# Linear attention and SwiGLU on one core: a fifth seven-product tile pair per chunk, 16-bit gating operands and a new issue order

## The chip, the cores and the metric

The kernel runs on one core of one Trainium2 chip. The metric is the device time in microseconds (us) of a whole execution. "Fast" is the state in which nearly all executions agree. Still, single executions of one kernel spread by about 1 us, and now and then one is 2 to 4 us longer at a lower granted clock. Where a median is given, the kernel before was run on the same chip. A profile shows a single execution, and not always a typical one.

## The reference

```python
# q, k, v: (8 batches, 8 heads, 576 positions, 64), fp32
q_s = softmax(q, axis=-1)                    # over the head dimension
k_s = softmax(k, axis=2)                     # over the positions
kv  = einsum('bhsd,bhse->bhde', k_s, v)
x   = einsum('bhsd,bhde->bhse', q_s, kv)     # -> 4608 tokens x 512
g   = x @ w_gate                             # 512 x 1536
u   = x @ w_val
out = (g * sigmoid(g) * u) @ w_out           # 1536 x 512, fp32
```

## The kernel before

TensorE (PE) does the matrix products. The first 576 tokens (the "head" of the program) run as plain products while batch 1's attention is made ready. "Chunk 0" has 448 tokens. Seven full chunks of 512 follow: 1 to 5 run one plan, 6 and 7 another, and a last output product ends the program.

In a chunk, gate and value tiles come in pairs of either of two forms. `Direct` does a pair of tiles with 16 matmuls of 512 columns. `Pair` does the same pair as a 2x2 block product with seven products instead of eight: 28 matmuls of 256 columns, paid for with sums of inputs (`xs`), sums of weights (`gt`), and adds and copies of its partial results on VectorE (DVE) and ScalarE (ACT). In steps `a` to `g` and `v`, `s1`, `s2` and `s5` are SBUF tiles that carry partial results:

```python
NP = 4                                  # pairs with ready weight sums
...
sn = ctx.enter_context(tc.tile_pool(name="sn", bufs=2))
...
def s_tile(self, nm):
    return sn.tile([128, 512], FP32, tag=nm, name=nm)[:, 0:2 * self.h]
...
elif step == "d":
    self.s2 = self.s_tile("s2")
    self.prod(self.x, self.sum(1), xs[1])
    copy(ceng, self.s2, self.x[:, 0:w])                        # ACT, or DVE with *
elif step == "e":
    self.prod(self.w, self.raw(wv, 1), xs[3])
    nc.vector.tensor_add(self.s2, self.w[:, 0:w], self.s2)     # in place, fp32
    meng.tensor_mul(self.out(0), self.halves(self.sa), self.halves(self.s2))  # POOL
...                                     # f and g do the same with s5
```

The gating product (`hr = silu(g) * u`) is mostly on GpSimd (POOL). The output product (`Quad`, steps A to H) uses the same seven-product form and the same tags `s1`, `s2`, `s5`, two buffers each.

The order of instructions on every engine is written by hand as a plan, a list of tokens (batch numbers start at 0, so batch 1 is the second):

```text
I, J      plain gate and value products of the head
O         half of an output product of the head, 6 matmuls of 512 columns
kk0:1     key-value product of batch 1, first half of the heads ("kv" on PE)
load:2    the last v load of the third batch, issued by SyncE (SP)
cv        cast of v on POOL      nm   norm of q on POOL, then a DMA transpose from SP
xx        the attention product "xa" of the next batch, which needs that transpose
Q, W, Y, X   sums of gate and value weights, of output weights, of this and of the next chunk's inputs
a..g,v    a Pair's steps         G, U a Direct's         a trailing * moves work to another engine
```

The head's plan and that of chunk 0 before:

```text
PLAN_B (head)
I0 I1 I2 I3 J0 J1 J2 I4 pe:1 J3 I5 I6 J4 I7 I8 J5 J6 J7 eq0:1 ns0:1 eq1:1 J8 I9 Q0
I10 I11 ek0:1 nd0:1* ns1:1 J9 J10 J11 nd1:1* O01 Q2* tr00 tr01 cv0:1 O02 tr10 Q1*
ek1:1 O11 kk0:1 O21 eq0:2 tr11 cv1:1 xz01 load:2 xz00 Q3 O12 kk1:1 ns0:2 O22 xz11*
O31 xz10 ek0:2 eq1:2 O32 nm0:2* cv0:2 cv1:2 ek1:2
PLAN_0 (chunk 0: four Pairs, two direct)
Y0 Y1 Y2 a0* G4 b0 c0 Y3* v0 G10 W0* a1 d0* U4 f0 G5 b1 ns1 c1 g0 e0 d1 v1 U10 a2
f1 nm1 e1 b2 v2 kv silu:2 g1 d2 c2 G11 f2 load e2 a3 g2 b3 c3 d3 v3 xx* W1 e3 f3
U5 U11 W3 X0 g3* X1 X2 W2 X3
```

The softmax here doesn't subtract the row's maximum and nothing guards it: scores larger than these inputs give would overflow.

Of the kernel before, what the change touches and what calls it, by code (L numbers as in the profile page):

```python
# [8 lines left out]
FP32 = mybir.dt.float32  # L9
# [7 lines left out]
def kernel(  # L17
# [19 lines left out]
    nc = tc.nc  # L37
# [10 lines left out]
    HM = MT // 2  # L48
    HN = d_model // 2
    XR = 1536  # L50
    NP = 4
    WARM = (64, 8, 8)

    const = ctx.enter_context(tc.tile_pool(name="const", bufs=1))
    ld = ctx.enter_context(tc.tile_pool(name="ld", bufs=3))
    at = ctx.enter_context(tc.tile_pool(name="at", bufs=2))
    ff = ctx.enter_context(tc.tile_pool(name="ff", bufs=4))
    ob = ctx.enter_context(tc.tile_pool(name="ob", bufs=5))
# [20 lines left out]

    def load(b, G, what, src, after=None):  # L80
        raw[what, b, G] = ld.tile(
            [128, 2, T * 64], FP32, tag=what, name=what, bufs=2 if what == "v" else 3
        )
        ap = bass.AP(
            tensor=src.tensor,
            offset=src[b, 4 * G].offset,
            ap=[[T * 64, 128], [2 * HSTR, 2], [1, T * 64]],
        )
        d = nc.sync.dma_start(out=raw[what, b, G], in_=ap)
        if after is not None:  # L90
            tc.add_manual_dep(d.ins, after.ins.name, SYNC, reason="order of loads")
        dmas[what, b, G] = d
# [207 lines left out]
    class First:  # L300
# [15 lines left out]
        def run(self, step, alt=False):  # L316
            if step == "I":
                ps = self.mm(wg, "g_ps")
                self.sg = ff.tile([128, S], FP32, tag="sg", name="sg")
                for p_, (c, n) in zip(ps, self.parts):  # L320
                    nc.scalar.activation(
                        out=self.sg[:, c:c + n], in_=p_[:, 0:n], func=AF.Silu
                    )
            else:
                for p_, (c, n) in zip(self.mm(wv, "u_ps"), self.parts):
                    nc.vector.tensor_mul(
                        hr[:, self.m, c:c + n], self.sg[:, c:c + n], p_[:, 0:n]
                    )
# [25 lines left out]
            eng.tensor_sub(s[3], a12, s[1])  # L354

    def sg_tile():
        return ff.tile([128, S], FP32, tag="sg", name="sg")

    class Pair:
        def __init__(self, c0, h, n, tsum, tc0):  # L360
# [29 lines left out]
                        start=first and j == 0 and kk == 0, stop=kk == 1, skip_group_check=True,  # L390
                    )

        def s_tile(self, nm):
            return sn.tile([128, 512], FP32, tag=nm, name=nm)[:, 0:2 * self.h]

        def run(self, step, alt=False):
            w = 2 * self.h
            ceng = nc.vector if alt else nc.scalar
            meng = nc.vector if alt else nc.gpsimd
            if step == "a":  # L400
                self.x, self.s1 = f_tile("sx"), self.s_tile("s1")
                self.prod(self.x, self.raw(wg, 0), self.xa(0, 0), True)
                copy(ceng, self.s1, self.x[:, 0:w])
            elif step == "b":
                self.y = f_tile("sy")
                self.prod(self.y, self.raw(wg, 1), self.xa(0, 1), True)
            elif step == "c":
                self.w, self.s5 = f_tile("sw"), self.s_tile("s5")
                self.prod(self.w, self.sum(0), xs[0], True)
                copy(ceng, self.s5, self.w[:, 0:w])  # L410
            elif step == "v":
                nc.vector.tensor_add(self.s1, self.y[:, 0:w], self.s1)  # L412
                self.sa = sg_tile()
                nc.scalar.activation(out=self.sa[:, 0:w], in_=self.s1, func=AF.Silu)  # L414
# [3 lines that stand above are left out]
                copy(ceng, self.s2, self.x[:, 0:w])  # L418
            elif step == "e":
                self.prod(self.w, self.raw(wv, 1), xs[3])  # L420
                nc.vector.tensor_add(self.s2, self.w[:, 0:w], self.s2)  # L421
                meng.tensor_mul(self.out(0), self.halves(self.sa), self.halves(self.s2))  # L422
            elif step == "f":
                self.prod(self.x, self.sum(2), xs[2])
                nc.vector.tensor_add(self.s5, self.x[:, 0:w], self.s5)  # L425
            elif step == "g":
                self.prod(self.x, self.sum(3), self.xa(1, 1))
                sb = sg_tile()
                nc.scalar.activation(out=sb[:, 0:w], in_=self.x[:, 0:w], func=AF.Silu)  # L429
                meng.tensor_mul(self.out(1), self.halves(sb), self.halves(self.s5))  # L430

    class Direct:
        def __init__(self, c0, n, m):
# [74 lines left out]
    class Quad:  # L508
        def __init__(self, Q, kks, own=False):
            self.Q, self.r, self.kks = Q, (512 * Q) % RING, kks  # L510
            pool = (lambda n: ld.tile([128, 512], FP32, tag=n, name="os")) if own else None
            self.s_tile = (
                (lambda n: pool("q" if n == "s1" else "k")) if own
                else lambda n: sn.tile([128, 512], FP32, tag=n, name=n)
            )
            self.o_sb = [[None, None], [None, None]]
# [83 lines left out]
    with tc.manual_schedule():  # L600
# [70 lines left out]
        def op(t, ci, c0, h, parts):  # L671
# [62 lines left out]
                g_sum(int(a), nc.vector if alt else nc.gpsimd)  # L734
            elif k == "T" and ci == B - 2:
                i = int(a)
                if i % 2 == 0:
                    parts["t"] = ld.tile(
                        [128, 2, 2, 2, 128 * (HM - NP)], FP16, tag=("q", "k")[i // 2], name="gt2"
                    )  # L740
                gt2[i] = parts["t"][:, i % 2]
                g_sum(i, nc.gpsimd if alt else nc.vector, 128 * NP, 128 * HM, gt2)

        def chunk(ci, c0, n, plan):
# [13 lines left out]
        ORDER = (0, 1, 2, 3, 4, 5)  # L758
        gt2 = [None] * 4
        PLAN_B = """  # L760
        I0 I1 I2 I3 J0 J1 J2 I4 pe:1 J3 I5 I6 J4 I7 I8 J5 J6 J7 eq0:1 ns0:1 eq1:1 J8 I9 Q0
        I10 I11 ek0:1 nd0:1* ns1:1 J9 J10 J11 nd1:1* O01 Q2* tr00 tr01 cv0:1 O02 tr10 Q1*
        ek1:1 O11 kk0:1 O21 eq0:2 tr11 cv1:1 xz01 load:2 xz00 Q3 O12 kk1:1 ns0:2 O22 xz11*
        O31 xz10 ek0:2 eq1:2 O32 nm0:2* cv0:2 cv1:2 ek1:2
"""
        PLAN_0 = """
        Y0 Y1 Y2 a0* G4 b0 c0 Y3* v0 G10 W0* a1 d0* U4 f0 G5 b1 ns1 c1 g0 e0 d1 v1 U10 a2
        f1 nm1 e1 b2 v2 kv silu:2 g1 d2 c2 G11 f2 load e2 a3 g2 b3 c3 d3 v3 xx* W1 e3 f3
        U5 U11 W3 X0 g3* X1 X2 W2 X3
"""  # L770
        PLAN = """
        S002 G4 pe a0 b0 A S222 S022 ek0 c0 S042 eq0 B S242 U4 d0 C ek1 S202 S142 eq1 v0
        S102 S122 e0 f0 a1* G10 S322 S302 D S342 b1 g0 cv0 cv1 v1 d1 ns1 E nm1 F c1 f1 a2
        U10 b2 ns0 c2 nm0 H* v2 g1 d2* e1 a3 f2 e2 b3 v3 kv c3 g2 d3 e3 G5 f3 xx X2 X0
        silu U5 G11 U11 load X1* X3 g3*
"""
        PLAN_N = """
        a0 S242 T0 b0 S022 A d0 S222 c0 v0 a1 f0 S002 S042 S102 S142 B g0 e0 d1 S122 b1 c1
        v1 a2 f1 b2 D S202 g1 T1 S302 d2 v2 e1 S322 c2 a3 f2 T2 C g2 d3 e2 b3 c3 T3* v3 f3
        a4 e3 b4 g3 d4 c4 v4 a5 S342 f4 b5 e4 g4 v5 d5* c5 E f5 e5 F g5* X0 X1 X3 X2 H*  # L780
"""
        PLAN_E = """
        S042 S002 A S102 S022 S242 S302 B C S122 S142 S322 S222 S342 D S202 E F H*
"""
        chunk(-1, 0, S, PLAN_B)
        chunk(0, S, 1024 - S, PLAN_0)
# [33 lines left out]
```

## Time and profile before

| | before |
|---|---|
| time, median of 3 runs | 298.43 us (298.03 to 298.5) |
| span of the profiled run | 296.2 us |
| head / chunk 0 / the rest / tail | 39.32 / 19.23 / 216.90 / 4.9 us |
| period of a steady chunk | 30.37 us |

The stretches are cut by PE's own instructions in the timeline. The head runs from the first plain gate product (15.89) to the first 224-column matmul of chunk 0 (55.21), chunk 0 to PE's first instruction of chunk 1 (74.44), the rest to the end of PE's last group (291.34), and the tail to the end of the span.

The page of the kernel before gives the span, then the busy time of each engine with its share and instruction count, then the shares of the chain of work that ended last:

```profile
span 296.2 us, 6921 instructions
...
PE 288.5 (97%) x2644; PEld 227.3 (77%) x2644; DVE 231.1 (78%) x496; ACT 207.2 (70%) x381; POOL 154.5 (52%) x121
...
PE 93%; DMA 3%; ACT 1%; DVE 0%; POOL 0%; issue 0%; ACTq 0%; DVEq 0%; POOLq 0%
```

PE is busy 97% of the span, and 93% of the chain is PE. The Trainium skill, "Trainium Kernel Development and Optimization", section "Performance Expectations", warns that matmul busy time is a bad metric for how close a kernel is to its bound, since matmuls are pipelined. So the bound is also checked by durations: in the steady chunk, 256-column matmuls start 0.109 us apart and 512-column ones 0.2155. "TensorE: Matmul & The Clock Gate", section "Wait — 56ns, not 53.3ns?", gives N / 2.4 GHz plus about 2.5 ns, which is 0.109 and 0.216: the trace agrees, so PE runs at its full rate there.

A steady chunk of the kernel before, by windows (start and end, length, busy us and instruction count of each engine, granted clock, DMA share, GB/s):

```profile
core 0: us, PE busy (x) PEld busy (x) DVE busy (x) ACT busy (x) POOL busy (x), PEclk, DMA share, GB/s
96.84:127.21 30.37, 30.37 (x282) 23.56 (x282) 25.45 (x56) 22.89 (x41) 16.30 (x13) 1.00 0.66 172
```

No engine but PE is full, and the clock is full. What PE waited for, over the whole of the kernel before (us in total, times, longest):

```profile
PE kv L192 <- POOL vb L118: 1.6, 1, 1.6
PE warm_ps L256 <- DVE zero L610: 1.1, 1, 1.1
```

The second is the start of the program. The first is in the head, as PE's timeline of the kernel before shows (start, us, engine, line, operation, out<-in, shapes, count, and in brackets the idle time before and what ended it):

```profile
42.91 1.46 PE L477 MATMUL o_ps<-wo,hr 128*128 128x512 f16 x6
45.95 0.70 PE L192 MATMUL kv<-vb,ek 64*128 64x129 bf16 x18 [1.59 <-POOL vb L118]
...
55.21 0.55 PE L388 MATMUL sx<-xt,wg 128*128 128x224 f16 x4
...
74.44 1.03 PE L439 MATMUL g_ps<-xt,wg 128*128 128x512 f16 x4
```

The first key-value product of batch 1 waits 1.59 us for POOL's cast of v, and the cast itself waits for a load. Chunk 0 follows at 55.21, chunk 1 at 74.44.

### The profile page before, as it was taken

Reading aid. Unit: us, or ns where it says so; the run is one execution under the profiler, and the core shown is the slowest. Engines: PE = TensorE matmul, PEld = TensorE weight load, DVE = VectorE, ACT = ScalarE, POOL = GpSimd, SP = SyncE. Lnnn points to the kernel's source line nnn. Section 1 sums busy time; section 2 is a strip of 40 time slices with the busy share of each in tenths; the row PEclk is TensorE's granted clock in tenths of the full one; section 3 lists DMA queues with packets and bytes.
Section 4 is the critical chain, followed back from the end, with each engine's and each line's share of the span. In section 5 each row is a group of like instructions: output and inputs, shape, how many; then the busy total and the mean of one; then the engine's idle time right before and its main releaser. Section 6 shows DMA issues by size and latency. Waiting matters only on the chain.

```text
span 296.2 us, 6921 instructions
## 1 busy us (share of the span) xinstructions
PE 288.5 (97%) x2644; PEld 227.3 (77%) x2644; DVE 231.1 (78%) x496; ACT 207.2 (70%) x381; POOL 154.5 (52%) x121
## 2 busy tenths in 40 slices
PE   8999997999999999999999999999999999999993
PEld 6877764587788678877887778767886888888882
DVE  2834785897997879787978798788889988787781
ACT  5667854968995589567966796679666785667441
POOL 1903737598029811991099109920893379147700
PEclk9999999999999999999999999999999999999998
DMA  7999999917705991579138913793351000600235
GB/s 261 291 190 243 244 308 362 340 25 231 289 2 109 158 395 45 90 159 393 65 73 169 388 73 74 152 342 138 73 117 36 2 0 13 133 2 0 64 80 142
DMA packets 38335, 46.43 MB, mean 157 GB/s; under 512 B 16288, under 2 KB 21408, under 8 KB 38304
## 3 DMA queue, kind: packets, MB, share of 16 engines
q1 hardware_dynamic: 32864, 41.03, 47.6%
q0 software_dynamic: 5280, 4.72, 10.1%
q8 instruction: 20, 0.33, 0.5%
q10 hardware_dynamic: 160, 0.26, 0.2%
q14 instruction: 11, 0.09, 0.1%
HBM read 37.75 MB, written 9.44 MB: 159 GB/s over the span
## 4 chain that ended last, share of the span: by engine, by line
PE 93%; DMA 3%; ACT 1%; DVE 0%; POOL 0%; issue 0%; ACTq 0%; DVEq 0%; POOLq 0%
PE sx L388 21%; PE ox L531 13%; PE sw L388 10%; PE u_ps L439 7%; PE ow L531 7%; PE g_ps L439 7%; PE sy L388 5%; PE g_ps L310 4%; PE warm_ps L256 4%; PE oy L531 4%; PE kv L192 3%; PE u_ps L310 3%; PE o_ps L477 2%; DMA v<-in_v_dram 2%; PE xa L273 1%; DMA out_dram<-o_sb 1%
## 5 line engine op out<-in xcount | busy, mean ns | idle before, releaser
L422 POOL TENSOR_TENSOR hr<-sg,s 128x512 bf16<-128x512 f32 (+1 forms) x36 | 46.0, 1284 | 63.7 <-ACT sg L414 47.0
L388 PEld LDWEIGHTS <-gt 128*128 128x128 f16 x576 | 55.7, 98 | 11.5 <-issue 1.1
L430 POOL TENSOR_TENSOR hr<-sg,s 128x512 bf16<-128x512 f32 (+1 forms) x28 | 36.2, 1292 | 21.2 <-ACT sg L429 21.0
L388 PE MATMUL sx<-xs,gt 128*128 128x256 f16 (+1 forms) x288 | 42.8, 271 | 0.1
L531 PEld LDWEIGHTS <-hs 128*128 128x128 bf16 x384 | 37.6, 98 | 5.4
L116 ACT COPY s<-sx 128x512 f32<-128x512 f32 (+1 forms) x58 | 33.7, 581 | 3.4 <-PE sx L388 2.8
L152 POOL TENSOR_TENSOR qs<-eq,rr 128x1152 bf16<-128x1152 bf16 x14 | 29.7, 2123 | 8.3 <-DVE rr L147 6.2
L388 PEld LDWEIGHTS <-wg 128*128 128x128 f16 x288 | 28.1, 98 | 6.0
L414 ACT ACTIVATE sg<-s 128x512 f32<-128x512 f32 (+1 forms) x36 | 22.6, 629 | 14.3 <-DVE s L412 12.3
L425 DVE TENSOR_TENSOR s<-sx,s 128x512 f32<-128x512 f32 (+1 forms) x36 | 24.5, 682 | 9.5 <-PE sx L388 5.5
L421 DVE TENSOR_TENSOR s<-sw,s 128x512 f32<-128x512 f32 (+1 forms) x36 | 24.4, 679 | 8.9 <-PE sw L388 4.6
L429 ACT ACTIVATE sg<-sx 128x512 f32<-128x512 f32 (+1 forms) x36 | 21.3, 592 | 13.8 <-PE sx L388 7.7
L531 PEld LDWEIGHTS <-hr 128*128 128x128 bf16 x288 | 28.2, 98 | 3.3
L116 ACT COPY s<-sw 128x512 f32<-128x512 f32 (+1 forms) x36 | 20.9, 581 | 12.5 <-PE sw L388 12.4
L412 DVE TENSOR_TENSOR s<-sy,s 128x512 f32<-128x512 f32 (+1 forms) x36 | 24.1, 669 | 1.6 <-PE sy L388 1.5
L143 DVE TENSOR_REDUCE rs<-eq 128x18 f32<-128x1152 bf16 x16 | 21.5, 1346 | 4.4 <-ACT eq L127 4.4
L439 PE MATMUL g_ps<-xt,wg 128*128 128x512 f16 (+1 forms) x96 | 24.2, 375 | 0.0
L439 PE MATMUL u_ps<-xt,wv 128*128 128x512 f16 (+1 forms) x96 | 24.1, 375 | 0.0
L531 PE MATMUL ox<-wt,hs 128*128 128x256 f16 x192 | 23.6, 273 | 0.0
L127 ACT ACTIVATE ek<-k 128x1152 bf16<-128x1152 f32 x16 | 18.8, 1172 | 6.7 <-DMA k<-in_k_dram 6.7
L127 ACT ACTIVATE eq<-q 128x1152 bf16<-128x1152 f32 x16 | 18.7, 1169 | 4.7 <-DMA q<-in_q_dram 4.7
L388 PE MATMUL sx<-xt,gt 128*128 128x256 f16 (+1 forms) x144 | 21.4, 271 | 0.1
(100 smaller groups left out, 581.7 us busy)
## 6 DMA issues: line engine op xcount, KB each, us to landing
q<-in_q_dram SPq DMA_DIRECT2D x16, 576.0 KB, 6.1
k<-in_k_dram SPq DMA_DIRECT2D x16, 576.0 KB, 6.3
v<-in_v_dram SPq DMA_DIRECT2D x16, 576.0 KB, 7.4
out_dram<-o_sb SPq DMA_DIRECT2D x70, 128.0 KB, 2.4
wv<-in_moe_w_val_dram POOLq DMA_DIRECT2D x3, 512.0 KB, 11.2
wo<-in_moe_w_out_dram POOLq DMA_DIRECT2D x3, 512.0 KB, 10.5
wg<-in_moe_w_gate_dram POOLq DMA_DIRECT2D x2, 512.0 KB, 11.2
wg<-in_moe_w_gate_dram POOLq DMA_DIRECT2D x2, 256.0 KB, 5.1
```

Of the source, the lines that this page charges most:

```text
L116: nc.scalar.copy(out=out, in_=in_)
L127: nc.scalar.activation(out=s["e" + what], in_=raw[what, b, G].rearrange("p h (t d) -> p t h d", d=64), func=AF.Exp,)
L152: eng.tensor_mul(s["qs"].rearrange("p t (h d) -> p (t h) d", d=64), s["eq"].rearrange("p t h d -> p (t h) d"), s["rr"].to_broadcast([128, ...
L388: nc.tensor.matmul(out=bank[:, h * j:h * j + h], lhsT=wgt(kk, j), rhs=rhs[:, kk, 0:h], start=first and j == 0 and kk == 0, stop=kk == 1, s ...
L412: nc.vector.tensor_add(self.s1, self.y[:, 0:w], self.s1)
L414: nc.scalar.activation(out=self.sa[:, 0:w], in_=self.s1, func=AF.Silu)
L421: nc.vector.tensor_add(self.s2, self.w[:, 0:w], self.s2)
L422: meng.tensor_mul(self.out(0), self.halves(self.sa), self.halves(self.s2))
L425: nc.vector.tensor_add(self.s5, self.x[:, 0:w], self.s5)
L430: meng.tensor_mul(self.out(1), self.halves(sb), self.halves(self.s5))
L439: nc.tensor.matmul(out=ps[:, 0:self.n], lhsT=w[:, kk, 128 * self.m:128 * self.m + 128], rhs=xt[:, kk, self.r:self.r + self.n], start=(kk = ...
L531: nc.tensor.matmul(out=dst[p][:, 0:HN], lhsT=lhs(kk, p), rhs=rhs(kk), start=start and i == 0, stop=i == HM - 1, skip_group_check=True,)
```

## The change

The intent: in chunks 0 to 5 a fifth pair takes the seven-product form, which is shorter on PE; the gating product gets two 16-bit operands, so that it is shorter on POOL and DVE; the space comes from one k buffer fewer; and all plans are written anew to fit.

```diff
-    NP = 4
+    NP = 5
@@ load
-            [128, 2, T * 64], FP32, tag=what, name=what, bufs=2 if what == "v" else 3
+            [128, 2, T * 64], FP32, tag=what, name=what, bufs=3 if what == "q" else None   # else 2
@@ sg_tile, and the same in First
-        return ff.tile([128, S], FP32, tag="sg", name="sg")
+        return ff.tile([128, S], FP16, tag="sg", name="sg")
@@ Pair
-        def s_tile(self, nm):
-            return sn.tile([128, 512], FP32, tag=nm, name=nm)[:, 0:2 * self.h]
+        def s_tile(self, nm, dt=FP32):
+            return sn.tile([128, 512], dt, tag=nm, name=nm)[:, 0:2 * self.h]
@@ step e
-                nc.vector.tensor_add(self.s2, self.w[:, 0:w], self.s2)
-                meng.tensor_mul(self.out(0), self.halves(self.sa), self.halves(self.s2))
+                u = self.s_tile("u0", FP16)
+                nc.vector.tensor_add(u, self.w[:, 0:w], self.s2)
+                meng.tensor_mul(self.out(0), self.halves(self.sa), self.halves(u))
@@ step f (step g then multiplies by self.u instead of self.s5)
-                nc.vector.tensor_add(self.s5, self.x[:, 0:w], self.s5)
+                self.u = self.s_tile("u1", FP16)
+                nc.vector.tensor_add(self.u, self.x[:, 0:w], self.s5)
@@ PLAN_B, the head
+        I0 I1 pe:1 I2 I3 J0 J1 I4 I5 J2 J3 J4 Q0 I6 J5 I7 J6 J7 eq0:1 ns0:1 eq1:1 I8
+        nd0:1* ns1:1 J8 I9 J9 I10 Q1* nd1:1* I11 cv0:1 tr00 J10 J11 tr10 ek0:1 O01 Q3*
+        cv1:1 ek1:1 O11 tr01 kk0:1 O02 tr11 eq0:2 O12 kk1:1 ns0:2 O21 xz10* ek0:2 xz00*
+        O22 Q2 xz01 eq1:2 cv0:2 xz11 O31 load:2 nm0:2 cv1:2 O32 ek1:2
@@ PLAN_0, chunk 0
+        a0 ns1 G5 b0 G11 Y0 c0 Y2 Y1 v0 Y3* d0* W2 a1 f0 b1 U5 c1 g0 d1 W0 v1 e0 a2 f1 b2
+        v2 kv silu:2 nm1 g1 d2 a3 e1 c2 f2 b3 c3 e2 g2 d3 v3 e3 a4 f3 xx* load g3 W1 d4*
+        b4 c4* X0 f4 v4 U11 e4* X2* X1 W3 X3 g4*
@@ cut: the plans of the full chunks and of the end, the tags of a wide tile and of the last Quads
```

More of the change, by code (lines that the diff above doesn't have):

```diff
@@ L50 @@
     XR = 1536
-    NP = 4
+    NP = 5
     WARM = (64, 8, 8)
     const = ctx.enter_context(tc.tile_pool(name="const", bufs=1))
-    ld = ctx.enter_context(tc.tile_pool(name="ld", bufs=3))
+    ld = ctx.enter_context(tc.tile_pool(name="ld", bufs=2))
     at = ctx.enter_context(tc.tile_pool(name="at", bufs=2))
@@ L318, in run @@
                 ps = self.mm(wg, "g_ps")
-                self.sg = ff.tile([128, S], FP32, tag="sg", name="sg")
+                self.sg = ff.tile([128, S], FP16, tag="sg", name="sg")
                 for p_, (c, n) in zip(ps, self.parts):
@@ L429, in run @@
                 nc.scalar.activation(out=sb[:, 0:w], in_=self.x[:, 0:w], func=AF.Silu)
-                meng.tensor_mul(self.out(1), self.halves(sb), self.halves(self.s5))
+                meng.tensor_mul(self.out(1), self.halves(sb), self.halves(self.u))
     class Direct:
@@ L510, in __init__ @@
             self.Q, self.r, self.kks = Q, (512 * Q) % RING, kks
-            pool = (lambda n: ld.tile([128, 512], FP32, tag=n, name="os")) if own else None
+            pool = (lambda n: ld.tile([128, 512], FP32, tag=n, name="os", bufs=3 if n == "q" else None)) if own else None
             self.s_tile = (
-                (lambda n: pool("q" if n == "s1" else "k")) if own
+                (lambda n: pool({"s1": "q", "s2": "v", "s5": "k"}[n])) if own
                 else lambda n: sn.tile([128, 512], FP32, tag=n, name=n)
@@ L736, in op @@
                 i = int(a)
-                if i % 2 == 0:
+                if i == 0:
                     parts["t"] = ld.tile(
-                        [128, 2, 2, 2, 128 * (HM - NP)], FP16, tag=("q", "k")[i // 2], name="gt2"
+                        [128, 4, 2, 2, 128 * (HM - NP)], FP16, tag="q", name="gt2", bufs=3
                     )
-                gt2[i] = parts["t"][:, i % 2]
+                gt2[i] = parts["t"][:, i]
                 g_sum(i, nc.gpsimd if alt else nc.vector, 128 * NP, 128 * HM, gt2)
@@ L760 @@
         PLAN_B = """
-        I0 I1 I2 I3 J0 J1 J2 I4 pe:1 J3 I5 I6 J4 I7 I8 J5 J6 J7 eq0:1 ns0:1 eq1:1 J8 I9 Q0
-        I10 I11 ek0:1 nd0:1* ns1:1 J9 J10 J11 nd1:1* O01 Q2* tr00 tr01 cv0:1 O02 tr10 Q1*
-        ek1:1 O11 kk0:1 O21 eq0:2 tr11 cv1:1 xz01 load:2 xz00 Q3 O12 kk1:1 ns0:2 O22 xz11*
-        O31 xz10 ek0:2 eq1:2 O32 nm0:2* cv0:2 cv1:2 ek1:2
+        I0 I1 pe:1 I2 I3 J0 J1 I4 I5 J2 J3 J4 Q0 I6 J5 I7 J6 J7 eq0:1 ns0:1 eq1:1 I8
+        nd0:1* ns1:1 J8 I9 J9 I10 Q1* nd1:1* I11 cv0:1 tr00 J10 J11 tr10 ek0:1 O01 Q3*
@@ L765 @@
+        cv1:1 ek1:1 O11 tr01 kk0:1 O02 tr11 eq0:2 O12 kk1:1 ns0:2 O21 xz10* ek0:2 xz00*
+        O22 Q2 xz01 eq1:2 cv0:2 xz11 O31 load:2 nm0:2 cv1:2 O32 ek1:2
 """
         PLAN_0 = """
-        Y0 Y1 Y2 a0* G4 b0 c0 Y3* v0 G10 W0* a1 d0* U4 f0 G5 b1 ns1 c1 g0 e0 d1 v1 U10 a2
-        f1 nm1 e1 b2 v2 kv silu:2 g1 d2 c2 G11 f2 load e2 a3 g2 b3 c3 d3 v3 xx* W1 e3 f3
-        U5 U11 W3 X0 g3* X1 X2 W2 X3
+        a0 ns1 G5 b0 G11 Y0 c0 Y2 Y1 v0 Y3* d0* W2 a1 f0 b1 U5 c1 g0 d1 W0 v1 e0 a2 f1 b2
+        v2 kv silu:2 nm1 g1 d2 a3 e1 c2 f2 b3 c3 e2 g2 d3 v3 e3 a4 f3 xx* load g3 W1 d4*
@@ L770 @@
+        b4 c4* X0 f4 v4 U11 e4* X2* X1 W3 X3 g4*
 """
         PLAN = """
-        S002 G4 pe a0 b0 A S222 S022 ek0 c0 S042 eq0 B S242 U4 d0 C ek1 S202 S142 eq1 v0
-        S102 S122 e0 f0 a1* G10 S322 S302 D S342 b1 g0 cv0 cv1 v1 d1 ns1 E nm1 F c1 f1 a2
-        U10 b2 ns0 c2 nm0 H* v2 g1 d2* e1 a3 f2 e2 b3 v3 kv c3 g2 d3 e3 G5 f3 xx X2 X0
-        silu U5 G11 U11 load X1* X3 g3*
+        a0 S042 b0 G5 c0 d0 A v0 S002 a1 f0 b1 S142 c1 v1 U5 S242 g0 pe S222 B S022 S102
+        S122 S302 d1 S322 ek0 e0 a2 S342 e1 eq0 ns0 S202 C ek1 f1 D E eq1 cv1 b2 c2* silu
@@ L776 @@
+        F nm0 cv0 g1 d2 v2 ns1 a3 nm1 H* f2 kv g2 d3 b3 c3 v3 e2 load f3 e3 a4 b4 c4 g3 v4
+        d4* e4 xx* f4 X2 G11 g4 X0 X1 X3* U11
 """
         PLAN_N = """
-        a0 S242 T0 b0 S022 A d0 S222 c0 v0 a1 f0 S002 S042 S102 S142 B g0 e0 d1 S122 b1 c1
-        v1 a2 f1 b2 D S202 g1 T1 S302 d2 v2 e1 S322 c2 a3 f2 T2 C g2 d3 e2 b3 c3 T3* v3 f3
-        a4 e3 b4 g3 d4 c4 v4 a5 S342 f4 b5 e4 g4 v5 d5* c5 E f5 e5 F g5* X0 X1 X3 X2 H*
+        a0 S222 b0 c0 d0 T0* A v0 S002 f0 a1 e0* S042 b1 g0 d1 c1 S022 v1 a2 f1 S242 S102
@@ L781 @@
+        b2 e1* c2 g1 S142 d2 v2 B f2 a3 T1* b3 c3 S342 S122 S202 g2* e2 d3 C S302 v3 f3
+        e3* S322 a4 b4 g3* d4 c4 v4 D T2 f4 e4* a5 b5 g4* c5* X0* d5 F f5 v5 E T3* X1 e5*
+        X3 g5* H* X2*
 """
         PLAN_E = """
-        S042 S002 A S102 S022 S242 S302 B C S122 S142 S322 S222 S342 D S202 E F H*
+        S022 A S042 S122 S002 S142 S202 B C S102 S302 S322 S242 S222 S342 D E F H*
 """
```

## The prediction

> **What bounds the kernel now.** TensorE: the chain of waits is 93% PE, the page has PE busy 97%, PE's own wait list holds 2.7 us, the granted clock is 0.995. In the timeline four 256-column matmuls start 0.437 us before what follows (0.109 each), four of 512 columns 0.862 (0.2155 each), four of 224 0.383, four of 448 0.754. Summed over a steady chunk (4 seven-product pairs, 2 direct pairs, 84 output matmuls, attention 1.7 us) this is 30.0 us; the trace's period is 30.37 (99.93 to 130.30), so about 0.3 us a chunk is stall. Other stalls: about 2.4 us in the head (kv(1,0) starts at 45.95, after a v load that landed at 44.76), 0.8 in chunk 0, 0.5 in each of the last two full chunks. A tail of 7 us is not touched. The other engines in a steady chunk (windows): DVE 25.4, ACT 22.9, POOL 16.3 us. None limits.
>
> **What the change does.**
> 1. A fifth pair in seven products in chunks 0 to 5: 28 x 0.109 = 3.06 us for 16 x 0.2155 = 3.45. It saves 0.39 us in five chunks and 0.34 in chunk 0: 2.3 us, all on the critical engine. Chunks 6 and 7 had six pairs already.
> 2. The others pay: per chunk three more PSUM copies on ACT (0.587 each), three more DVE adds (0.69) for two fewer gate multiplications (0.685), and half of the x evictions moves from DVE to ACT (about 1.5 us). ACT goes to about 26 of 30 us, DVE to about 24.7: they fit, with less slack.
> 3. The gating product in 16 bits: on POOL about 1.15 us for 1.29 (a 16-bit POOL subtraction of this shape took 1.15), on DVE about 0.42 for 0.69 (as its 16-bit sums). The Trainium skill, "VectorE: DVE Perf Modes", section "What auto-detection actually checks", says that DVE takes its two-per-cycle mode when every tensor is 16-bit; 0.42 against 0.69 us in this trace agrees. POOL doesn't limit, so this is worth nearly nothing in time.
> 4. Two k buffers: the third batch's k load must now wait for the exponent of the second's k, which ended before that load was issued. About 0; it pays for the space of wider weight sums.
> 5. Weight sums a quarter wider (POOL 2.12 to about 2.65 us each), where POOL waits on DMA. About 0.
> 6. The new order. kv(1,0) now comes after two output halves instead of three, while its load is set by DMA: that stall grows by about 1.3 us unless the load comes sooner. In the steady chunk six x evictions on ACT (about 3 us) stand before the next chunk's first direct product, with about 0.5 us of slack: 0 to 0.5 us lost per chunk, or the new order recovers the 0.3 lost now. Net +0.3 us, very uncertain.
>
> **Sum.** 298.4 - 2.3 + 0.3 = 296.4 us; range 293.6 to 299.0. Faster by over 2%: 0.04; within 2%: 0.93; slower: 0.03.
>
> **What would show it.** Step 1: 72 more matmuls, a steady period of 29.9 to 30.2 us. Step 2: ACT near 26 us in it. Step 3: POOL's product at 1.15, DVE's at 0.42 us. Step 6: PE idle before kv(1,0) near 2.9 us (now 1.6), chunk 0's first pair at 56 us (now 55.2).
>
> **What would make it wrong.** A PE stall at each chunk boundary (late x evictions), PSUM banks short around the attention products, or a POOL product slower in 16 bits: +1 us a chunk gives 301. Or an order that removes most of the 6 us of stalls: 292.

## The result, and the profile after

No change was measured. The kernel after took 298.33 us (median of 4 runs, 298.07 to 299.05), the kernel before in the same rounds 298.23 (297.67 to 298.5). All outputs are right. The ratio is 1.001, with a 95% interval of 0.9986 to 1.0033. A ratio here is from the fast runs of both kernels, so not quite the ratio of the medians that are quoted. 298.33 lies inside the predicted range of 293.6 to 299.0, which was wide enough to hold no gain at all; the predicted gain of 2 us isn't there.

The page of the kernel after:

```profile
span 297.2 us, 7118 instructions
...
PE 285.4 (96%) x2716; PEld 233.2 (78%) x2716; DVE 240.9 (81%) x490; ACT 221.6 (75%) x416; POOL 157.3 (53%) x128
...
PE 72%; DMA 1%; ACT 0%; ACTq 0%; DVE 0%; issue 0%; DVEq 0%
```

PE has 72 more matmuls and 3.1 us less work, yet the span didn't shrink. The chain's shares need care: they add up to 73% only, because it was followed back to the attention product of chunk 0 at 73.5 us, and no further. The fall from 93% to 72% is no finding.

A steady chunk of the kernel after, by windows:

```profile
97.31:127.28 29.97, 29.97 (x294) 24.67 (x294) 26.42 (x53) 25.34 (x49) 19.25 (x15) 1.00 0.56 165
```

The chunk did become 0.40 us shorter, and the helpers fit under PE. So the gain is there, and something else gives it back. What PE waited for, over the whole of the kernel after:

```profile
PE g_ps L310 <- ACT sg L321: 1.5, 1, 1.5
PE kv L192 <- POOL vb L118: 1.4, 1, 1.4
PE xa L273 <- DVE wt L492: 1.3, 1, 1.3
PE warm_ps L256 <- DVE zero L612: 1.1, 1, 1.1
PE tp L168 <- DVE qs L152: 0.5, 1, 0.5
PE sx L388 <- DVE s L118: 0.3, 1, 0.3
PE kv L192 <- DVE vb L118: 0.2, 1, 0.2
```

There are five waits more than before. By PE's timeline, those for `tp` (at 10.6) and for `vb` on DVE (at 13.7) lie ahead of the head; the others lie in the head and in chunk 0. Cutting both traces at the same instructions says how much went where. The predicted column is worked out from the prediction's steps. Its net of +0.3 for the order, with 1.3 us lost before the key-value product, implies 1.0 won back; the only such gain that it names is the 0.3 us of stall in each steady chunk.

| stretch, us | before | after | difference | predicted |
|---|---|---|---|---|
| start of the program to the head | 15.89 | 15.64 | -0.25 | 0 |
| head | 39.32 | 41.06 | +1.74 | +1.3 |
| chunk 0 | 19.23 | 20.89 | +1.66 | -0.34 |
| chunk 1 to PE's last group | 216.90 | 214.32 | -2.58 | -1.95, and -1.0 "recovered" |
| tail | 4.9 | 5.3 | +0.4 | 0 |
| span | 296.2 | 297.2 | +1.0 | -2.0 |

The two spans are single runs, and their difference of 1.0 is larger than that of the medians (0.1). But the stretches repeat: a second profile of the unchanged kernel after (the control below) has 41.10 and 20.83 for the head and chunk 0.

PE's timeline of the kernel after, in the head and at the end of chunk 0:

```profile
34.38 1.14 PE L310 MATMUL u_ps<-xt,wv 128*128 128x320 f16 x8
37.07 2.26 PE L310 MATMUL g_ps<-xt,wg 128*128 128x320 f16 x16 [1.54 <-ACT sg L321]
...
41.99 2.75 PE L479 MATMUL o_ps<-wo,hr 128*128 128x512 f16 x12
...
46.37 0.70 PE L192 MATMUL kv<-vb,ek 64*128 64x129 bf16 x18 [1.40 <-POOL vb L118]
...
56.70 0.55 PE L388 MATMUL sx<-xt,wg 128*128 128x224 f16 x4
...
73.54 0.33 PE L273 MATMUL xa<-qtd,kn 64*64 64x320 bf16 x4 [1.26 <-DVE wt L492]
...
77.59 0.60 PE L388 MATMUL sx<-xt,wg 128*128 128x256 f16 x4
```

The product waits at nearly the same time as before (46.37 against 45.95), and in both traces POOL starts the cast at 44.76, when the load has landed. The date of v is set by DMA and didn't move between these two profiles. The new order has one output half less to do before that date and one more after it. It also inserts a wait of 1.54 us for ACT, which has the exponents of q ahead of the silu that frees the PSUM tile. The two waits sum to 2.94 us, against 1.59 before. The one for ACT is hardly a loss of its own: what PE doesn't wait there, it waits for v. In the second profile of this kernel the two took 0.87 and 2.43 us, and the head was as long (41.10). The head's 1.74 can be cut at the key-value product. Up to it, 0.67 us are lost: the head starts 0.25 us sooner while v's date stays, and POOL's cast takes 1.56 us instead of 1.14. After it, 1.07 us are lost, where one output half (1.3 us of PE work) more has to be done.

In chunk 0 the attention product `xa` waits 1.3 us (the list's third line). The list names DVE as its releaser. Where that engine had long been done, the last to come was another, so follow the operand: `xa` reads the transposed q, and SP's own list of issues gives it away. The kernel before:

```profile
49.59 1.30 SPq L466 DMA_DIRECT2D out_dram<-o_sb  x2
50.93 0.67 SPq L89 DMA_DIRECT2D v<-in_v_dram  x1
51.65 5.48 SPq L466 DMA_DIRECT2D out_dram<-o_sb  x6
```

The kernel after:

```profile
49.55 6.21 SPq L468 DMA_DIRECT2D out_dram<-o_sb  x6
55.86 0.53 SPq L89 DMA_DIRECT2D v<-in_v_dram  x1
...
68.54 1.30 SPq L180 DMA_TRANSPOSE qtd<-qs  x1
```

The v load now stands behind six output stores instead of two. SP issues in order, and a store is issued only once its data is ready. The Trainium skill, "DMA: Bandwidth & Descriptors", section "Anatomy of one DMA — SWDGE (gpsimd) path", says that any semaphore wait happens on the issuing sequencer before dispatch. That section is about DMAs from POOL, but this trace shows the same on SP: one issue takes 0.47 to 0.61 us, some 3.4 for six, and the stretch of six takes 6.21, so the rest is waiting. The load goes out 4.9 us later than before. POOL's timeline of the kernel after, in chunk 0, shows what hangs on it:

```profile
60.79 1.65 POOL L118 CAST vb<-v 128x1152 bf16<-128x1152 f32 x1 [3.66 <-DMA v<-in_v_dram]
...
66.39 2.12 POOL L152 TENSOR_TENSOR qs<-eq,rr 128x1152 bf16<-128x1152 bf16 x1
```

The cast comes at 60.79 (before: 57.49) and the norm of q, behind it in POOL's order, ends at 68.5. Then SP issues the transpose, and about 5 us later, at 73.54, `xa` starts.

The 16-bit operands did what was predicted of their durations. The product's groups, the kernel before (line, engine, operation, shapes, count, busy us, mean ns of one, idle before and releasers):

```profile
L422 POOL TENSOR_TENSOR hr<-sg,s 128x512 bf16<-128x512 f32 x32 | 41.5, 1302 | 62.7 <-ACT sg L414 47.0 <-DVE s L412 11.7 <-DVE s L421 4.0
L430 DVE TENSOR_TENSOR hr<-sg,s 128x512 bf16<-128x512 f32 x7 | 4.8, 688 | 1.3 <-ACT sg L429 1.3
```

The kernel after:

```profile
L423 POOL TENSOR_TENSOR hr<-sg,u 128x512 bf16<-128x512 f16 x27 | 31.6, 1179 | 22.6 <-DVE u L422 21.9 <-ACT xt L116 0.2
L423 DVE TENSOR_TENSOR hr<-sg,u 128x512 bf16<-128x512 f16 x10 | 4.3, 426 | 1.0
```

(A line shows the type of the first input alone.) POOL needs 1.18 us for 1.30, DVE 0.43 for 0.69. The Trainium skill, "VectorE: DVE Perf Modes", section "What auto-detection actually checks", gives DVE's two-per-cycle mode to instructions whose tensors are all 16-bit, and the trace agrees. DVE is nevertheless 1.0 us a chunk busier than before, where the prediction had it 0.7 us less busy. Some of its sums of `hr` became slower, as this stretch of the kernel after shows:

```profile
91.64 1.10 DVE L506 TENSOR_TENSOR hs<-hr 128x512 bf16<-128x512 bf16 x1
```

Others of the same shape take about 0.41 us. The Trainium skill, "SBUF — State Buffer", section "Who interferes with whom", says that a DVE instruction with two SBUF inputs contends with a GpSimd instruction that reads SBUF, and calls the port pair that they share an exclusive lock. POOL was in its cast of v here, from 91.33 to 92.47, and DVE's sum ended 0.27 us after it, so the trace agrees; no run tests it by itself, and DVE doesn't limit in the steady chunks.

### The profile page after: what moved, and what is told of

Read it like the earlier page. It is cut to its first block, busy times and chain, and to the rows that moved or that the text cites. A ratio compares the mean times of both kernels' runs of the same rounds, so it can differ in the third digit from the quotient of the medians.

```text
span 297.2 us, 7118 instructions
## 1 busy us (share of the span) xinstructions
PE 285.4 (96%) x2716; PEld 233.2 (78%) x2716; DVE 240.9 (81%) x490; ACT 221.6 (75%) x416; POOL 157.3 (53%) x128
## 4 chain that ended last, share of the span: by engine, by line
PE 72%; DMA 1%; ACT 0%; ACTq 0%; DVE 0%; issue 0%; DVEq 0%
PE sx L388 23%; PE ox L533 13%; PE sw L388 11%; PE ow L533 7%; PE sy L388 6%; PE oy L533 4%; PE u_ps L441 3%; PE g_ps L441 3%; PE kv L192 2%; PE xa L273 1%; DMA out_dram<-o_sb 1%; PE xz L273 0%; ACT o_sb L116 0%; ACTq L468 0%; DVE o_sb L553 0%
## 5 line engine op out<-in xcount | busy, mean ns | idle before, releaser
L432 POOL TENSOR_TENSOR hr<-sg,u 128x512 bf16<-128x512 f16 (+1 forms) x33 | 39.1, 1184 | 51.8 <-ACT sg L431 50.8
L116 ACT COPY s<-sx 128x512 f32<-128x512 f32 (+1 forms) x77 | 44.3, 577 | 7.7 <-PE sx L388 7.4
L423 POOL TENSOR_TENSOR hr<-sg,u 128x512 bf16<-128x512 f16 (+1 forms) x31 | 36.5, 1184 | 23.1 <-DVE u L422 22.3
L427 DVE TENSOR_TENSOR u<-sx,s 128x512 f16<-128x512 f32 (+1 forms) x42 | 28.5, 680 | 9.8 <-ACT sg L414 4.0
L414 ACT ACTIVATE sg<-s 128x512 f16<-128x512 f32 (+1 forms) x42 | 26.3, 625 | 12.8 <-DVE s L412 11.0
L431 ACT ACTIVATE sg<-sx 128x512 f16<-128x512 f32 (+1 forms) x42 | 25.2, 600 | 10.7 <-PE sx L388 10.6
L422 DVE TENSOR_TENSOR u<-sw,s 128x512 f16<-128x512 f32 (+1 forms) x42 | 28.4, 677 | 2.5 <-PE sw L388 1.2
L388 PE MATMUL sw<-xs,wv 128*128 128x256 f16 (+1 forms) x168 | 24.9, 271 | 0.0
L388 PE MATMUL sx<-xt,wg 128*128 128x256 f16 (+1 forms) x168 | 24.9, 271 | 0.0
L388 PE MATMUL sy<-xt,wg 128*128 128x256 f16 (+1 forms) x168 | 24.9, 271 | 0.0
L388 PE MATMUL sw<-xs,gt 128*128 128x256 f16 (+1 forms) x168 | 24.9, 271 | 0.0
```

The costliest lines, as they stand in the source:

```text
L116: nc.scalar.copy(out=out, in_=in_)
L388: nc.tensor.matmul(out=bank[:, h * j:h * j + h], lhsT=wgt(kk, j), rhs=rhs[:, kk, 0:h], start=first and j == 0 and kk == 0, stop=kk == 1, s ...
L414: nc.scalar.activation(out=self.sa[:, 0:w], in_=self.s1, func=AF.Silu)
L422: nc.vector.tensor_add(u, self.w[:, 0:w], self.s2)
L427: nc.vector.tensor_add(self.u, self.x[:, 0:w], self.s5)
L431: nc.scalar.activation(out=sb[:, 0:w], in_=self.x[:, 0:w], func=AF.Silu)
```

## The experiments

Two theories were set against each other. A: the arithmetic gains what was predicted, and the new order of the head and of chunk 0 gives it back. B: chunk 0 loses because a fifth pair doesn't fit there in any order, or because the narrower operands cost something.

### The load earlier, the old head, an older chunk 0

Kernel early_v is the kernel after with the v load issued sooner in the head:

```diff
- ... tr01 kk0:1 O02 tr11 ... O31 load:2 nm0:2 ...
+ ... tr01 kk0:1 load:2 O02 tr11 ... O31 nm0:2 ...
```

> The kernel after with one step moved in the first plan: the load of the third batch's second v is issued before the third output half instead of behind seven of eight. Theory A (the gain of the fifth pair is there in the steady chunks, 0.40 us each, and is given back in the head and chunk 0 by the new order; the late v load, issued at 55.9 us, landing 60.8, delays POOL's cast, Y3, the gate products and nm1, so the second transpose lands at 73.5 and the attention product waits 1.3 us for it): 296.6 to 297.5 us, the wait before the attention product in chunk 0 under 0.4 us, the cast of v at about 58 us. Theory B (the 16-bit operands[...] or the extra load of the fifth pair take the gain back; the order matters little): 298.0 to 298.6, as the kernel after. Theory C (the wait is for DVE's W1, as the profile's wait list names it): the wait of 1.3 us stays, 298.0 to 298.6.

Measured: 298.79 us against 298.54, ratio 1.0004 (0.9953 to 1.0055). Chunk 0 was 20.52, only 0.4 shorter, and `xa` still waited 1.0 us for the transpose. As the whole cause in the kernel after, the load's place falls: something else also delays the transpose. POOL's timeline names it: the cast of v ends at 60.3, but the norm stands behind two gate products, and POOL waits 4.31 us for ACT's silu before the first of them. The profiled run is the slowest of the six (301.88). The head was 44.20 us here, with a wait of 2.88 us before the key-value product and a granted clock of half speed for some 3 us after it.

Kernel old_head is the kernel after with the head's plan (`PLAN_B`) of before.

> The kernel after with the whole first plan (head) of the kernel before. Theory A: the first pair of chunk 0 comes 1.1 to 1.7 us sooner than in the kernel after and the v load is early again, so chunk 0 is shorter by 1 us or more: 295.2 to 296.4 us. Theory B: 298.0 to 298.6.

Measured: 301.27 us, ratio 1.0097 (1.0046 to 1.0148). The head came back to 39.19, so the head's loss is the order's. But chunk 0 grew to 22.25, with a new wait of 1.5 us for the input sums that DVE makes at its start. DVE comes to these sums late, behind a norm of q that the old head gives it (1.47 us at 54.23); so the new chunk 0 seems to count on the new head's order. The tail was 7.5 us in this profile, for a store's issue that took 2.94 us instead of 0.56; that wasn't explained.

Kernel old_c0 has a chunk 0 made by hand from the plan of before, with a fifth pair put in; old_both has that and the old head.

```diff
+ Y0 Y1 Y2 a0* G5 b0 c0 Y3* v0 G11 W0* a1 d0* U5 f0 b1 ns1 c1 g0 e0 d1 v1 U11 a2
+ f1 nm1 e1 b2 v2 kv silu:2 g1 d2 c2 f2 load e2 a3 g2 b3 c3 d3 v3 e3 a4 f3 xx* W1
+ b4 c4 g3* d4 W3 v4 e4 f4 X2 g4* X0 X1 W2 X3
```

> The kernel after with the second plan (chunk 0) of the kernel before, the fifth pair put in for its direct pairs by hand; the head stays the new one, with its late v load. Theory A: no gain, and perhaps up to 2 us worse, since POOL has a W sum of 3.1 us in that plan behind the late cast, and nm1 behind both: 298 to 300.5 us. Theory B: within 0.5 of the kernel after. If the second plan alone were at fault, whatever the head does: 296.0 to 297.0.

Measured: 303.85 us, ratio 1.0147 (1.01 to 1.0195); chunk 0 took 24.86.

> The kernel after with head and chunk 0 of the kernel before (fifth pair put in by hand). Theory A: all of the 3.4 us that the traces show lost before chunk 1 come back, less what my hand-made chunk 0 loses: 294.8 to 296.0 us, with a steady period of 29.97 us. Theory B: 298 or more.

Measured: 301.47 us, ratio 1.0078 (1.0035 to 1.0121); head 39.58, chunk 0 23.66. In both, PE waits 1.9 us for one of DVE's adds and 1.6 to 1.8 us for ACT's copies. These two say little of the change: a plan put together by hand brings waits of its own. That is a lesson on such experiments, too.

### Four pairs in chunk 0, five after it

Kernel c0_four is the kernel after with both `PLAN_B` and `PLAN_0` of before, word for word: four pairs in chunk 0, five from chunk 1 on.

> The kernel after with the head and chunk 0 of the kernel before word for word, so chunk 0 has four pairs and two direct ones again, and the fifth pair starts in chunk 1. Theory A2 (formed after the first four runs: from chunk 1 on every version takes 214.3 us against 216.9 before, while head and chunk 0 together take 61.4 to 63.2 against 58.5; the fifth pair and the wider weight sums don't fit into chunk 0, where DVE and ACT are bunched): head and chunk 0 together at most 59.3 us, 295.6 to 296.8 us in all, ratio to the kernel before 0.990 to 0.995. Theory B (the 16-bit operands or the load of the change cost the gain everywhere): 298 or more.

Measured: 297.31 us (296.22 to 298.81) against 298.15, ratio 0.9968 (0.9928 to 1.0008). The stretches are those of theory A: head 39.49, chunk 0 19.23, the rest 214.80. In the whole time the gain isn't clear of noise in this run. By their clock the executions fall in two bunches, four at 296.2 to 298.0 (0.995 to 0.997) and two at 298.8 (0.991 and 0.992), so the median shows only part of it.

Kernel early_nm is early_v with POOL's norm of q moved ahead as well:

```diff
- a0 ns1 G5 ... v0 Y3* d0* ... v2 kv silu:2 nm1 g1 ...
+ a0 ns1 G5 ... v0 Y3* nm1 d0* ... v2 kv silu:2 g1 ...
```

> The kernel after with the v load early and nm1 of the third batch put ahead of the first gate product in POOL's order. Theory A3 (in chunk 0 the attention product waits for the second transpose because nm1 stands behind two gate products in POOL's in-order queue, not because of the v load): the wait of 1.0 to 1.3 us before it goes below 0.3, chunk 0 takes 19.5 to 20.2 us against 20.9, 297.0 to 298.0 us in all. If DVE's load is what limits chunk 0, the time of chunk 0 stays within 0.4 us of 20.9.

Measured: 299.17 us, ratio 1.0032 (1.0 to 1.0064). In chunk 0 the wait for the transpose is gone, and the chunk takes 19.88: 1.0 less than in the kernel after, but still 0.65 more than with four pairs. PE's listed waits in it are 0.33 us for a copy on DVE and 0.25 for a sum on DVE. The head ate the gain: 42.41. After the wait of 2.41 us for v, the windows of early_nm show the clock:

```profile
44.00:46.00 2.00, 0.00 (x0) 0.00 (x0) 1.44 (x3) 0.23 (x1) 1.64 (x1) 1.00 1.01 378
...
49.00:50.00 1.00, 1.00 (x7) 0.58 (x6) 0.19 (x1) 0.61 (x2) 1.00 (x1) 0.50 1.05 355
51.00:52.00 1.00, 1.00 (x21) 0.53 (x18) 0.00 (x0) 0.53 (x2) 1.00 (x2) 1.00 1.01 378
```

The second figure from the left in each row is the window's length, and the third from the right the granted clock. PE idles around 44 to 46, runs at half the clock at 49 to 50, and is back by 51. So a wait there can cost more than its own length.

### What the 16 bits are for

Kernel before_16 is the kernel before with the changed `sg_tile`, `s_tile` and steps e, f and g, and nothing else of the change.

> The kernel before with the gating product in 16 bits alone. Theory A2: nothing on the critical path changes, POOL's product 1.18 for 1.29 us: within 0.3 us of the kernel before. Theory B: 0.5 us or more slower.

Measured: 297.68 us (297.04 to 298.06) against 298.15, ratio 0.9974 (0.9941 to 1.0008): the same time within the error. The narrower operands cost nothing by themselves, which takes the second half of theory B away.

Kernel after_32 takes them out of the kernel after. The adds write back into `s2` and `s5`, as before, in 32 bits:

```diff
-        return ff.tile([128, S], FP16, tag="sg", name="sg")
+        return ff.tile([128, S], FP32, tag="sg", name="sg")
-                u = self.s_tile("u0", FP16)
+                u = self.s2
-                self.u = self.s_tile("u1", FP16)
+                self.u = self.s5
```

> The kernel after with the gating product back in 32 bits. Theory A2: POOL and the few products on DVE take longer (1.29 and 0.69 us), hidden in the steady chunks: 298.0 to 299.0 us, steady period within 0.1 of 29.97. Theory B: faster than the kernel after by 0.5 us or more. If the 16 bits are needed to make the new order fit: 300 or more.

Measured: 325.62 us, ratio 1.0915 (1.0876 to 1.0955). A steady chunk of after_32, by windows:

```profile
99.67:134.32 34.65, 31.76 (x295) 25.45 (x294) 26.40 (x54) 26.16 (x50) 21.30 (x16) 0.95 0.52 151
```

The chunk takes 34.65 us, 4.68 more than in the kernel after. PE is not busy for 2.9 of them; the other 1.8 are work at a lower clock (0.95 in the mean), since the clock fell to half after the wait. What the engines of after_32 waited for:

```profile
DVE s L118 <- POOL hr L432: 20.8, 5, 4.2
...
PE ox L533 <- DVE o_sb L553: 14.6, 5, 3.1
```

DVE's timeline of after_32 at such a place:

```profile
124.90 0.74 DVE L553 TENSOR_TENSOR o_sb<-ow,s 128x256 f32<-128x256 f32 x2
129.81 0.69 DVE L118 COPY s<-sw 128x512 f32<-128x512 f32 x1 [4.17 <-POOL hr L432]
```

In the kernel after, the same two stand right behind each other:

```profile
93.27 0.74 DVE L553 TENSOR_TENSOR o_sb<-ow,s 128x256 f32<-128x256 f32 x2
93.93 0.68 DVE L118 COPY s<-sw 128x512 f32<-128x512 f32 x1
```

The copy into a buffer of `s5` must wait until POOL has read the previous content, and POOL is late. DVE stands still for 4.17 us, then PE waits for DVE, once a chunk. In the kernel after the sum goes into a tile of its own, so that `s5` is free when DVE's add has read it. The plan of the full chunks has the copy (`c2*`) ahead of the product (`g1`) that would hold its buffer, whatever the width: in the kernel after POOL runs that product from 95.77 to 96.93, 3.0 us after the copy has started. So an in-place sum in this order would cost about 3 us of waiting in 16 bits, too (an estimate from this trace; not run).

Is it the width or the separate tile? Kernel own_u32 has the separate tiles `u0` and `u1` in 32 bits; the gate's operand `sg` stays in 16:

```diff
-                u = self.s_tile("u0", FP16)
+                u = self.s_tile("u0", FP32)
-                self.u = self.s_tile("u1", FP16)
+                self.u = self.s_tile("u1", FP32)
-    bufs=3 if what == "q" else None          # and in the two other places that use the tag q
+    bufs=None                                # two q buffers: room for the wider tiles
```

> The kernel after with the value operand of the gating product in 32 bits again, but in tiles of its own as in the kernel after (room for it is made with two q buffers in place of three). Theory L, buffer life (the run with everything in 32 bits took 325 us because there the DVE sum is written back into the s2 and s5 tiles, which POOL's late product then holds, so a copy on DVE waits 4.2 us per chunk; the 16 bits matter only because they make room for tiles of their own): 298.0 to 299.8 us, no waits of DVE's copies for POOL's product. Theory W, width (the 32-bit operand itself is what the new order can't stand): 305 us or more.

Measured: 302.62 us, ratio 1.0107 (1.0072 to 1.0142), which misses what was expected. But the steady chunk, from 129.49 to 159.47, takes 29.98 us, as in the kernel after, and no copy waits for POOL. So in the steady chunks it is the separate tile that counts, not the width of `u`. (POOL's product took 1.19 us here, so this run doesn't test a slower POOL; the order of `c2*` and `g1` above does not depend on it.) The profiled run is the slowest of seven (305.08): its head took 42.9 us, for after a wait of 2.34 us for v the clock fell to half for about 3 us. The loss that all the runs share is in the last two full chunks, which take 4.2 us longer than in the kernel after. There PE waits for DVE's adds, as in own_u32:

```profile
242.59 0.60 PE L388 MATMUL sy<-xt,wg 128*128 128x256 f16 x4 [0.59 <-DVE s L412]
```

And at the same place of after_32:

```profile
262.46 0.60 PE L388 MATMUL sy<-xt,wg 128*128 128x256 f16 x4 [0.76 <-DVE s L412]
```

The kernel after has no such wait. The q buffer that own_u32 lacks isn't needed for it, since after_32 has three. What the two share is the 32-bit operand: 18 of DVE's products in these chunks take 0.69 and 0.79 us on average instead of 0.43 and 0.53. So there the width counts, as far as these two runs show; no run changes it by itself. The q buffer had to go because the kernel doesn't build otherwise: the tiles would need 20 KB a partition, where 17 KB are left. With 16-bit tiles it is 16 KB. The narrow operands are also what makes the separate tiles fit.

### The head alone, and a chunk 0 with less waiting

Kernel head_O is the kernel after with one output half moved ahead of the key-value product; after_fix has that and the norm of q early, as in early_nm; fill_kv is c0_four with an output half moved ahead of it.

```diff
- ... O11 tr01 kk0:1 O02 tr11 ...           # head_O, after_fix
+ ... O11 tr01 O02 kk0:1 tr11 ...
- ... O11 kk0:1 ... Q3 O12 kk1:1 ...        # fill_kv
+ ... O11 O12 kk0:1 ... Q3 kk1:1 ...
```

> The kernel after with one step moved in the head: the second half of the first output tile before the first kv product instead of after it. Theory O (the start of kv(1,0) is set by the v load and POOL's cast; what counts is how much TensorE work stands after it): wait before kv at most 0.4 us, chunk 0's first pair 1.0 to 1.4 us sooner, 296.9 to 297.6 us. If the stall of 1.5 us before I10 (ACT busy with the exponents) were a loss of its own: within 0.4 us of the kernel after.

Measured: 298.33 us against 299.12, ratio 0.9967 (0.9935 to 0.9999). The head took 40.43, 0.6 less, where 1.0 or more was expected. PE no longer waits before the first key-value product, which starts at 46.20; but it waits 0.46 us before the second one, for POOL's cast of the next v, which also waits for its load. So the loads limit the head at more than one place.

> The kernel after with two steps moved: the same output half before kv, and nm1 of the third batch ahead of the first gate product in chunk 0. Theory O and A3 together: 295.8 to 296.8 us; chunk 0 takes at most 20.1 us.

Measured: 298.46 us, ratio 0.9972 (0.994 to 1.0003), which misses. Chunk 0 stayed at 20.70. The wait for the transpose went, and PE waited 0.9 us for a copy on ACT instead. Unlike early_nm, this kernel has the late load; so the early norm alone doesn't shorten chunk 0.

> The version with the head and chunk 0 of the kernel before (c0_four) with one more output half moved ahead of the first kv product. Theory O: the wait before kv goes from 1.8 to below 0.6 us and chunk 0 starts about 1 us sooner; 295.0 to 296.3 us, and less spread between runs, since the runs of c0_four at 298.8 had a lower granted clock (0.991 against 0.996), as after waits of 2.4 us and more before kv in two other traces, where the clock fell to 0.50 for about 3 us. If DMA sets the end of the head: no gain over c0_four.

Measured: 297.63 us, ratio 0.9951 (0.9915 to 0.9988), as c0_four within the error, and worse by its stretches (head 40.61, chunk 0 21.12): the moved half is missing later, and PE then waits before the second key-value product (0.44) and in chunk 0. The move also puts the last v load behind four stores instead of two (it goes out at 54.08), and in chunk 0 `xa` waits 0.97 us for the transpose, beside 0.69 for DVE's input sums: a like loss with the old head and four pairs.

### A control, a filler, and the load's place by itself

Kernel after_again is the kernel after, unchanged.

> The kernel after unchanged, as the control on this chip. All theories: 298 to 299 us, ratio to the kernel before 0.998 to 1.003.

Measured: 298.49 us against 298.88, ratio 0.999 (0.9957 to 1.0023): the result holds. Its wait for v was 2.4 us, and this time the clock did not fall.

Kernel newhead_four has the new head (as in head_O) and the chunk 0 of before with four pairs.

> The new head (with the output half ahead of kv, as in head_O) and chunk 0 of the kernel before with four pairs. If the five pairs and the new plan of chunk 0 cost the time there: chunk 0 about 19.3 us as in c0_four, 296.2 to 297.2 us in all. If the late loads of the new head do: chunk 0 20.5 us or more, 298 or more.

Measured: 299.03 us, ratio 1.0002 (0.997 to 1.0034). Chunk 0 took 21.10 us, where the same plan behind the old head takes 19.23. The fifth pair isn't needed for the loss. Kernel nh4_early differs from it in one token, `load:2`:

```diff
- ... O02 kk0:1 tr11 ... O31 load:2 nm0:2 ...
+ ... O02 kk0:1 load:2 tr11 ... O31 nm0:2 ...
```

> newhead_four with the v load issued before the stores. If the late load is the cause: POOL's cast of that v by 57.5 us, no wait for the transpose, chunk 0 at most 19.6 us against 21.1, 297.0 to 297.8 us in all. If not: chunk 0 20.5 us or more.

Measured: 297.84 us (297.36 to 299.03) against 299.51, ratio 0.9932 (0.9888 to 0.9977), and chunk 0 at 19.57. SP's issues in newhead_four:

```profile
49.55 5.65 SPq L468 DMA_DIRECT2D out_dram<-o_sb  x6
55.30 0.54 SPq L89 DMA_DIRECT2D v<-in_v_dram  x1
```

And in nh4_early:

```profile
49.95 1.18 SPq L468 DMA_DIRECT2D out_dram<-o_sb  x2
51.18 0.59 SPq L89 DMA_DIRECT2D v<-in_v_dram  x1
```

PE's timeline of newhead_four at the attention product, a wait that isn't there in nh4_early:

```profile
74.22 0.33 PE L273 MATMUL xa<-qtd,kn 64*64 64x320 bf16 x4 [1.10 <-DMA qtd<-qs]
```

With four pairs, then, the place of one load behind four more stores costs chunk 0 1.5 us. That is shown by one profile of each; the medians differ by 1.2. They were run at other times.

Kernel c0_four_warm is c0_four with ten filler matmuls (256 columns of zeros, 1.25 us) in front of the key-value product, where PE waits anyway; before_warm is the kernel before with the same filler.

```diff
- ... O11 kk0:1 O21 ...
+ ... O11 wu:1 kk0:1 O21 ...      # wu: ten matmuls into an unused PSUM tile
```

> The version with head and chunk 0 of the kernel before and the fifth pair from chunk 1 on (c0_four), with ten filler matmuls ahead of the first kv product of the second batch, where TensorE waits anyway. If the high runs of c0_four (298.8 at clock 0.991) come from the clock falling after that wait: all runs at 296.0 to 297.0 us, clock 0.995 or more, ratio to the kernel before 0.990 to 0.995. If not: the same two groups as c0_four.

Measured: 296.38 us (296.13 to 297.01) against 298.88, ratio 0.9918 (0.9887 to 0.995). Its page has a span of 294.2 us and PE busy for 98% of it.

> The kernel before with the same filler. If its high runs (299.5 to 301.8) come from that wait: no run above 299.2, the low ones unchanged within 0.4 us. If not: the same spread as before.

Measured: 298.75 us (298.05 to 299.83), ratio 0.9999 (0.9965 to 1.0033). In the kernel before, the filler changes nothing.

The best version was run once more as best_again.

> c0_four_warm once more: 296.0 to 297.0 us, ratio to the kernel before 0.989 to 0.995.

Measured: 297.11 us (296.12 to 300.73; the highest, at a clock of 0.991, counts as slow, and the five fast ones have a median of 296.83) against 299.51, ratio 0.9907 (0.9859 to 0.9954). So the best version is 0.8 to 0.9% faster than the kernel before, twice, with intervals that exclude no change. How much of that is the filler's isn't shown: c0_four without it has 0.9968, and the intervals overlap. That it doesn't remove every slow run, best_again shows.

## Why the prediction was wrong

**Right: the steady chunks (step 1).** 72 more matmuls came, as said. The period went from 30.37 to 29.97, 0.40 saved for 0.39 predicted.

**Right but for a size: what the others pay (step 2), and the products' durations (step 3).** ACT came to 25.3 us for 26, DVE to 26.4 for 24.7; nothing waits for that in steady chunks. POOL's product took 1.18 us for 1.15, DVE's 0.43 for 0.42. That before_16 ran in the same time confirms "worth nearly nothing in time" for the old order.

**Wrong in role: the narrower operands.** The prediction saw only their speed. They make separate tiles fit, and without those the new order loses 27 us (after_32). With separate tiles in 32 bits the steady chunk is as short as with 16 bits, but the last two full chunks take 4.2 us longer, where PE waits for DVE, whose products are slower in 32 bits (own_u32). So with the new order the speed on DVE counts, too.

**The step that failed: "It saves 0.39 us in five chunks and 0.34 in chunk 0: 2.3 us, all on the critical engine", together with "Net +0.3 us" for the order in step 6.** For the head, step 6 had the mechanism and nearly the size: 1.3 us more waiting was predicted, 1.35 came, and the stretch grew by 1.74. Before the key-value product PE idles 1.40 us, not 2.9; the other 1.54 come just earlier, behind ACT's exponents, and would else be waited for v. With the plan of before the head returns to 39.2 to 39.5 us (old_head, c0_four).

For chunk 0, step 6 priced nothing, and step 1 booked a gain of 0.34. It cost 1.66 (20.89 us for 19.23): an error of 2.0 us, the largest in the sum. The overlap was wrong: PE's work there isn't all that is on the critical path, since `xa` waits for a transpose that hangs on SP's and POOL's order. The wait for the transpose (1.26) and one of 0.33 for a copy on DVE are the listed part of it. The 1.0 us that was to be won back elsewhere came to about 0.6, and in the last two full chunks: the steady period fell by 0.40, the arithmetic alone, so the 0.3 of stall that step 6 hoped for didn't come back. Together with the tail, which grew by 0.4 for reasons not looked into, this accounts for the missing gain.

**Why chunk 0 lost.** The new head puts a v load behind six stores in SP's order, and late with it are POOL's cast, the norm behind it, the transpose and the attention product. That is shown for four pairs: 21.10 us with the load late, 19.57 with it early. For five pairs it is only a part. The early load alone gave 0.4 us (early_v), the early norm alone nothing (after_fix), both together 1.0 (early_nm, one profile). The best chunk 0 with five pairs took 19.88 us, the one with four 19.23. No run of five pairs showed the saving of 0.34 us, and what limits it there, after the transpose is early, stays open. A copy on ACT is the wait that after_fix turned up.

**What the gain needed.** With four pairs and the old plans in the head and in chunk 0, and five pairs after it, the gain of the steady chunks arrives: head 39.49, chunk 0 19.23, the rest 214.80 for 216.90.

## What to carry to other kernels

Price a new order stretch by stage: the ramp-up has other limits than the steady chunks, and a saving that holds in five chunks may turn into a loss in the one that starts them. Before a load in an issue queue is moved, look at what stands ahead of it there: a store waits for its data, and the load behind it waits too. A narrower type can matter by the buffers that it makes room for, and its speed can count in one stage while it is worth nothing in the others.

## What the Trainium skill lacked or had wrong

- "TensorE: Matmul & The Clock Gate", section "What's actually happening": it puts the fall to half clock after at least one idle window of about 3.4 us. Here the clock fell to 0.50 after shorter waits: 2.34 us (own_u32), 2.41 (early_nm), 2.88 (early_v) and four of 2.9 in after_32. It did not fall after one of 2.43 (after_again) and one of 3.07 (after_32), so the length alone doesn't decide. It stayed at half for some 3 us, in after_32 once for 6.
- "GPSIMD Engine Reference": its time for a two-input operation is in fp32 only. Here POOL's product took 1.30 us with 32-bit inputs and 1.18 with 16-bit ones (128x512, the output in bf16 in both), so narrow inputs gain 9% on POOL, where they gain 38% on DVE (0.69 to 0.43). With one input in 16 bits and one in 32 (own_u32) POOL took 1.19 and DVE 0.69.
- No page that was used says that an in-place sum ties a tile to its slowest reader on another engine. Here that made the difference between steady chunks of 30.0 and 34.7 us.
